# Attention and token mixing: the first batch planned with other durations, priorities and shares of work

## The chip, the cores and the metric

One NeuronCore of a Trainium2 chip runs the whole program. The metric is the device time of one execution in microseconds; lower is better. TensorE (PE) multiplies, with its weight loads (PEld) beside it; VectorE (DVE) and ScalarE (ACT) work on its results, GpSimd (POOL) issues most loads and casts a little, SyncE (SP) issues the remaining loads and the stores.

## The reference

For 4 batches, 8 heads, 768 positions and 64 columns a head, it computes attention with sinks and a window, and puts the result through a token and channel mixer:

```python
scores = scale * np.matmul(q, k.transpose(0, 1, 3, 2))
keep = is_sink | in_window              # 4 sinks; the last 128 positions
a = softmax(np.where(keep, scores, -1e9))
x = np.matmul(a, v)                     # heads side by side: [4, 768, 512]
h = np.maximum(x^T @ w_tok1, 0) @ w_tok2      # 768 -> 256 -> 768
u = x + h^T
out = u + np.maximum(u @ w_ch1, 0) @ w_ch2    # 512 -> 1536 -> 512
```

Inputs and output are float32; the kernel works in bfloat16 and accumulates in float32.

## The kernel before

**Tiling.** Two heads make a pair: 4 pairs a batch, 16 in all, numbered from 0. For a pair, q and k are turned by PE (`turn` in the first batch and for pair 4, `transposed` later) and copied out of PSUM as qT and kT; the four sink columns of k go to kTs (`sink_columns`). `scores` makes the window's scores in three groups a pair, g = 0, 1, 2: two of 512 columns a head and one of 384. ACT takes the exp of each (line 509), giving pT. `score_sinks` makes the sink scores of two pairs at once. `pv` multiplies with v, with a column of ones that gives the row sum; DVE takes the reciprocal (572, 612) and writes x (575, 615).

**Mixing.** Per batch and half of the columns g: `mix_h` (x by w_tok1, then relu to h1T), `mix_u` (h1T by w_tok2, plus x, gives u), `transpose_u` or `turned_u` (u turned to uT). Then `mix_channels`: `v1` (uT by w_ch1, relu, line 122 or 124) and `out_part` (by w_ch2, plus u, line 884, stored).

**Masks.** A score group is masked in one of two ways. By PE: `masked` multiplies a table of 0 and -32768 by the identity into the bank, and the scores accumulate on it. By DVE: after the exp, pT is multiplied by a table of 0 and 1 (line 516), which `keep_masks` makes in four instructions (1005). In the first batch PE masks all groups but group 0 of pair 3.

**u.** In the first batch `mix_u` has two forms as well: with `by_pe`, x is added by a product with the identity, and the result only copied, by ACT or DVE; otherwise DVE adds x while it reads the bank (716). Four of the six pieces of the first batch are `by_pe`.

**Banks.** PSUM has two slots "sc", of two banks each, for scores and for turned q and k, and four single banks "mx" for all else. A slot is free for PE when all its readers are done.

**The order.** Every engine works its queue in order, and the order is written when the program is built, by a planner (`Plan`). Each unit of PE work and each operation (`Op`) has an assumed duration per engine it may run on. The planner keeps a clock per engine, and gives the operation that can start earliest to the engine that would finish it first; between equals `urgent` decides. `SEM` is added behind an operation until its result counts as seen, `PE_OUT` behind a PE unit, `SWITCH` where PE changes between work on half the array and on all of it. In the first batch the lists that `first_attention` returns have priority in their order (`stay` and the 40 ns in line 322 say how much later an item high in the list may start and still be taken first). Behind it, `main` (channel mixing) and `side` (attention and token mixing of the next batch) are woven; `target` says how much of the side must be done at which share of main (0.6 in line 1025). Assumed landings of the first loads stand in `landed(...)` (977, 980, 1009). None of these numbers is in the program that runs: they only decide which engine takes what, the order in each queue, and the bank.

**Bursts.** In the later batches the turning of the next pair's q and k, the scores of group 0 and the sinks' part of the last pair's values stand together as one burst; groups 1 and 2 follow in a second one, with channel mixing as filler between the two.

**Loads.** q and k of pairs 0 to 3 come by SP in float32 and are cast on chip (`cast`); everything else comes by POOL, cast on the way, in one fixed sequence: v of pairs 0 to 2, w_tok1, v of pair 3, w_tok2, then pairs 4 and on, with quarters of w_ch1 and w_ch2 between them.

Of the kernel before, what the change touches and what calls it, by code (L numbers as in the profile page):

```python
# [16 lines left out]
def kernel(  # L17
# [16 lines left out]
    NT = S // P  # L34
# [12 lines left out]
    MASKED_BY_PE = [(p, g) for p in range(NHP) for g in range(NT // 2) if (p, g) != (NHP - 1, 0)]  # L47
# [164 lines left out]
    SEM = 90.0  # L212
    PE_OUT = 190.0
    SWITCH = 95.0
    FIRST = 1800.0
# [22 lines left out]
    class Plan:  # L238
# [71 lines left out]
        def run(self, first, main, side, target):  # L310
# [3 lines left out]
            while any(first) or main or side or self.pending:  # L314
# [4 lines left out]
                if early:  # L319
                    soonest = min(t for t in [tm, ts, *(t for t, _ in early)] if t is not None)  # L320
                    stay = [(t, u) for t, u in early if self.half and u[0].half and t <= soonest + SWITCH]
                    t, u = next((e for e in stay + early if e[0] <= soonest + (SWITCH if e in stay else 40.0)), (None, None))
# [71 lines left out]
    def prepare(p):  # L394
# [4 lines left out]
        def evict(e, n, part):  # L399
# [8 lines left out]
            copy(e, to if parts == 1 else to[:, part], tiles["ps_" + name, p] if parts == 1 else tiles["ps_" + name, p][part])  # L408

        def sink_columns(e):  # L410
            c = ODD * (p % 2)
            first = (tiles["ps_k", p][:, 0] if parts == 1 else tiles["ps_k", p][0])[:, 0, 0:n_sink]
            for i in range(2):
                copy(e, ks[ds(D * i, D), i, c:c + n_sink], first[ds(D * i, D)])

        free = ([("sk", p - 2)] if p >= 2 else [], [("s", p - NKB)] if p >= NKB else [])
        if parts == 2:
            cost = {"DVE": 540.0, "ACT": 500.0}
        else:
            cost = {"DVE": 950.0} if p < NHP else {"DVE": 950.0, "ACT": 900.0}  # L420
        for n, name in enumerate(("qT", "kT")):
# [7 lines left out]
            {"ACT": 440.0, "DVE": 400.0}, sink_columns, [("sk", p - NHP)] if p >= NHP else [],  # L429
        )  # L430

    def turn(p, n):
# [3 lines left out]
        def run():  # L436
            ps = [bank("mx", NT, D, dtype=BF16) for _ in range(2)]
            tiles["ps_" + name, p] = [t.rearrange("d j p -> d p j") for t in ps]
# [47 lines left out]
    def scores(p, g):  # L486
# [32 lines left out]
        x.cost, x.fn, x.deps = {"ACT": 190.0 + 1.5 * width(g)}, exp, [done["pv", p - 2]] if p >= 2 else []  # L519
        x.urgent = 2 * (p < NHP)  # L520
        then = [x]
        if not by_pe:
            then.append(Op({"DVE": 100.0 + 1.2 * width(g)}, mask, [x, done["masks"]]))
# [6 lines left out]
    def score_sinks(p):  # L530
# [13 lines left out]
        x = Op({"ACT": 580.0}, exp, [done["pv", p - 2]] if p >= 2 else [])  # L544
# [6 lines left out]
    def pv(p, half):  # L551
# [29 lines left out]
        r = Op({"DVE": 180.0}, recip)  # L581
        n = Op({"DVE": 550.0}, norm, [r])
        n.urgent = r.urgent = (1 + 1.5 * (p >= NHP // 2)) * (p < NHP)
# [9 lines left out]
    def sink_values(p):  # L593
# [15 lines left out]
        for i in range(2):  # L609
# [10 lines left out]
            done["r", p, i] = Op({"DVE": 180.0}, recip)  # L620
            done["x", p, i] = Op({"DVE": 550.0}, norm, [done["r", p, i]])
# [19 lines left out]
    def sink_rows(p):  # L641
# [5 lines left out]
        done["vs", p] = Op({"ACT": 440.0, "DVE": 400.0}, both, [done["v", p], done["pv", p - NHP]])  # L647
# [422 lines left out]
```

## Time and profile before

| | us |
|---|---|
| median of 3 runs (lowest to highest) | 209.58 (209.21 to 210.65) |
| the profiled execution: time | 209.46 |
| its span, first to last instruction | 207.7 |
| PE busy in the span | 198.0 (95%) |
| DVE busy | 114.3 (55%) |
| ACT busy | 114.4 (55%) |
| POOL busy | 67.5 (32%) |
| w_tok1 landed (first token product at 19.27) | 19.22 |
| last exp of the first batch ends | 22.95 |
| first product with w_ch1 | 30.78 |

The span runs from the first to the last instruction; 1.76 us of the time lie outside it. All later times are microseconds from the start of the span. Busy times of PE are modelled, as matmuls are pipelined: the row of a 256-column product says 0.27 us, but the next one starts 0.11 us later. Where work follows on work, the step from start to start is what an instruction costs its engine, and the row is what its reader waits for. The granted TensorE clock is 0.998 of full speed over the whole span.

### The profile page before, as it was taken

The numbers are of one execution on the slowest core, as the hardware profiler recorded it, in microseconds if no ns is written. First come the engines' busy times: TensorE is split into PE (matmuls) and PEld (weight loads), VectorE is DVE, ScalarE is ACT, GpSimd is POOL, SyncE is SP. The second block draws the span as 40 slices with busy tenths as digits, with TensorE's granted clock in tenths as the row PEclk, the third lists the DMA queues.
The fourth block names the chain that finished last, engine by engine and source line by source line (L and its number), as shares of the span: only waits on it lengthen the run. The fifth ranks groups of instructions, "written<-read, shape, count | busy, mean of one in ns | idle before, by whom it ended". The sixth has DMA issues, their size and how long they took to land.

```text
span 207.7 us, 5034 instructions
## 1 busy us (share of the span) xinstructions
PE 198.0 (95%) x2126; PEld 119.3 (57%) x2145; DVE 114.3 (55%) x252; ACT 114.4 (55%) x202; POOL 67.5 (32%) x86
## 2 busy tenths in 40 slices
PE   6699999999999999999999999999999999999994
PEld 2345975566665665557656645666666445665443
DVE  4786664777577675867576552767674421000222
ACT  4799668878727435867684241868751103774000
POOL 6399759794699980720000000000000000000000
PEclk9999999999999999999999999999999999999999
DMA  6999999999999999795000212100001122000222
GB/s 198 283 260 182 172 174 191 156 164 201 156 159 176 185 206 195 52 70 37 3 0 5 101 51 104 51 5 0 3 0 49 56 101 101 3 0 0 101 104 101
DMA packets 73222, 21.57 MB, mean 104 GB/s; under 512 B 63216, under 2 KB 70256, under 8 KB 73200
## 3 DMA queue, kind: packets, MB, share of 16 engines
q0 software_dynamic: 67232, 11.80, 71.9%
q1 hardware_dynamic: 5968, 9.45, 12.9%
q8 instruction: 17, 0.28, 0.6%
q14 instruction: 5, 0.04, 0.1%
HBM read 26.75 MB, written 6.29 MB: 159 GB/s over the span
## 4 chain that ended last, share of the span: by engine, by line
PE 83%; DMA 6%; DVE 4%; ACT 2%; issue 2%; POOL 1%; SPq 0%; POOLq 0%; DVEq 0%
PE ps_mx L109 75%; PE ps_sc L109 5%; DMA w_tok<-in_moe_w_tok_dram 4%; DMA v_sink_f<-in_v_dram 2%; PE ps_sc L460 2%; DVE x_sb L615 1%; ACT qT L116 1%; DVE kT L118 1%; POOL v_aug L102 1%; PE ps_mx L745 1%; ACT v1T L122 1%; DVE recip L612 1%; PE ps_mx L112 1%; POOL v_sink L118 0%; SPq L188 0%
## 5 line engine op out<-in xcount | busy, mean ns | idle before, releaser
L109 PE MATMUL ps_mx<-uT,w_ch 128*128 128x384 bf16 x384 | 68.3, 326 | 0.9 <-DVE x_sb L615 0.9
L109 PE MATMUL ps_mx<-w_ch,v1T 128*128 128x512 bf16 (+2 forms) x299 | 64.2, 362 | 0.9 <-issue 0.3
L122 ACT ACTIVATE v1T<-ps_mx 128x384 bf16<-128x384 f32 x74 | 36.3, 493 | 33.7 <-PE ps_mx L109 22.9
L109 PEld LDWEIGHTS <-w_ch 128*128 128x128 bf16 x384 | 35.5, 98 | 25.0 <-DVE x_sb L615 2.5
L109 PEld LDWEIGHTS <-v1T 128*128 128x128 bf16 x312 | 28.9, 98 | 29.2
L509 ACT ACTIVATE pT<-ps_sc 128x1024 bf16<-128x1024 f32 (+1 forms) x48 | 44.4, 956 | 2.2 <-PE ps_sc L109 1.9
L884 DVE TENSOR_TENSOR o_sb<-ps_mx,u_sb 128x512 f32<-128x512 f32 x23 | 15.9, 691 | 44.6 <-PE ps_mx L109 44.6
L94 POOL DMA_DIRECT2D q_bf<-in_q_dram x24 | 19.7, 822 | 4.7 <-DMA w_ch<-in_moe_w_ch_dram 2.4
L109 PEld LDWEIGHTS <-w_tok 128*128 128x128 bf16 x192 | 18.3, 98 | 4.8 <-DMA w_tok<-in_moe_w_tok_dram 0.5
L94 POOL DMA_DIRECT2D k_bf<-in_k_dram x24 | 19.6, 820 | 3.1 <-DMA w_ch<-in_moe_w_ch_dram 1.7
L102 POOL DMA_DIRECT2D v_aug<-in_v_dram x16 | 16.4, 1028 | 10.9 <-PE ps_mx L109 8.0
L118 DVE COPY kT<-ps_sc 128x768 bf16<-128x768 bf16 x11 | 10.5, 958 | 17.0 <-ACT qT L116 17.0
L516 DVE TENSOR_TENSOR pT<-pT,mask_main 128x1024 bf16<-128x1024 bf16 (+1 forms) x24 | 14.5, 620 | 3.6 <-ACT pT L509 3.5
L109 PE MATMUL ps_sc<-qT,kT 64*128 64x256 bf16 x192 | 15.5, 262 | 0.3
L109 PE MATMUL ps_mx<-v_aug,pT 128*128 128x65 bf16 x352 | 15.3, 194 | 0.0
L716 DVE TENSOR_TENSOR u_sb<-ps_mx,x_sb 128x512 bf16<-128x512 f32 x20 | 12.7, 685 | 4.2 <-PE ps_mx L109 4.2
L109 PEld LDWEIGHTS <-pT 128*128 128x128 bf16 x352 | 13.5, 97 | 2.0 <-issue 0.6
L124 DVE TENSOR_SCALAR v1T<-ps_mx 128x384 bf16<-128x384 f32 x22 | 12.1, 554 | 2.7 <-PE ps_mx L109 2.0
L109 PE MATMUL ps_mx<-h1T,w_tok 128*128 128x256 bf16 x96 | 12.6, 273 | 0.0
L116 ACT ACTIVATE qT<-ps_sc 128x768 bf16<-128x768 bf16 x11 | 8.9, 810 | 6.4 <-PE ps_sc L460 6.2
L109 PE MATMUL ps_mx<-x_sb,w_tok 128*128 128x256 bf16 x96 | 12.0, 273 | 0.1
L615 DVE TENSOR_TENSOR x_sb<-ps_mx,recip 128x384 bf16<-128x384 f32 x22 | 11.4, 551 | 0.1
(72 smaller groups left out, 152.2 us busy)
## 6 DMA issues: line engine op xcount, KB each, us to landing
out_dram<-o_sb SPq DMA_DIRECT2D x23, 256.0 KB, 2.0
v_aug<-in_v_dram POOLq DMA_DIRECT2D x16, 192.0 KB, 6.5
w_ch<-in_moe_w_ch_dram POOLq DMA_DIRECT2D x8, 384.0 KB, 8.9
q_bf<-in_q_dram POOLq DMA_DIRECT2D x24, 96.0 KB, 6.6
k_bf<-in_k_dram POOLq DMA_DIRECT2D x24, 96.0 KB, 5.6
q_f<-in_q_dram SPq DMA_DIRECT2D x4, 384.0 KB, 5.6
k_f<-in_k_dram SPq DMA_DIRECT2D x4, 384.0 KB, 5.9
w_tok<-in_moe_w_tok_dram POOLq DMA_DIRECT2D x2, 384.0 KB, 8.1
```

Source lines behind the costliest of these rows:

```text
L94: in_order(nc.gpsimd.dma_start(out=out[:, h], in_=rows[:, h]))
L102: in_order(nc.gpsimd.dma_start(out=v_aug.rearrange("p i t d -> p (i t) d")[:, :, 0:D], in_=v[b].rearrange("h s d -> (h s) d")[2 * hp * S:2 ...
L109: in_order(nc.tensor.matmul(*args, skip_group_check=True, **kwargs))
L116: in_order(nc.scalar.activation(out, in_, AF.Copy))
L118: in_order({"DVE": nc.vector, "POOL": nc.gpsimd}[e].tensor_copy(out=out, in_=in_))
L122: in_order(nc.scalar.activation(out, in_, AF.Relu))
L124: in_order(nc.vector.tensor_scalar_max(out=out, in0=in_, scalar1=0.0))
L509: in_order(nc.scalar.activation(part(tiles["pT", p][:, :, ds(2 * g, 2)]), tiles["ps_s", p, g][:, :, 0:width(g)], AF.Exp, scale=scale,))
L516: in_order(nc.vector.tensor_tensor(out=pt, in0=pt, in1=m, op=ALU.mult))
L615: in_order(nc.vector.tensor_tensor(out=x_sb[b][:, :, ds((2 * hp + i) * D, D)], in0=tiles["ps_o", p, i][:, :, 0:D], in1=tiles["recip", p, i ...
L716: in_order(nc.vector.tensor_tensor(out=u_part(b, g, s0, n), in0=tiles["ps_u", b, g, s0], in1=x_sb[b][:, s0:s0 + n, c0:c0 + cn], op=ALU.add,))
L884: in_order(nc.vector.tensor_tensor(out=o_sb.rearrange("p (g c) -> p g c", g=2), in1=u_rows(b, st), in0=tiles["ps_out", b, st].rearrange("p ...
```

## The change

Three things change in what is computed where, all in the first batch:

- DVE masks three groups (pair 2 group 2, pair 3 groups 0 and 2) in place of one; PE masks nine in place of eleven.
- u of the first batch is added by DVE in all six pieces; `mix_u` loses its form with the identity, so four copies that ACT made go too.
- The lists of `first_attention` are returned in another order: the token work of the second half of the columns stands second, ahead of the masks.

All else is numbers of the planner: durations of operations are set to about the step from one instruction to the next (an exp 100 + 1.62 a column for 190 + 1.5, a copy of 384 columns 470 and 400 for 540 and 500), the delay behind an operation grows (`SEM` 165 for 90) and the one behind PE shrinks (`PE_OUT` 45 for 190), a new `STAY` of 250 takes the place of `SWITCH` in the two tests for first lists, urgency of exps and norms is changed, landings of loads are set anew (the tables of `keep_masks` count as ready at 18.0 us for 5.7), and `target` has 0.7 for 0.6. The parts of a turned pair in `tiles` get keys of their own, which changes nothing in the program.

The diff, without the lines around each place:

```diff
@@ line 47 of before @@
-    MASKED_BY_PE = [(p, g) for p in range(NHP) for g in range(NT // 2) if (p, g) != (NHP - 1, 0)]
+    MASKED_BY_DVE = [(NHP - 2, 2), (NHP - 1, 0), (NHP - 1, 2)]
@@ line 212,2 of before @@
-    SEM = 90.0
-    PE_OUT = 190.0
+    SEM = 165.0
+    PE_OUT = 45.0
@@ line 214,0 of before @@
+    STAY = 250.0
@@ line 321,2 of before @@
-                    stay = [(t, u) for t, u in early if self.half and u[0].half and t <= soonest + SWITCH]
-                    t, u = next((e for e in stay + early if e[0] <= soonest + (SWITCH if e in stay else 40.0)), (None, None))
+                    stay = [(t, u) for t, u in early if self.half and u[0].half and t <= soonest + STAY]
+                    t, u = next((e for e in stay + early if e[0] <= soonest + (STAY if e in stay else 100.0)), (None, None))
@@ line 408 of before @@
-            copy(e, to if parts == 1 else to[:, part], tiles["ps_" + name, p] if parts == 1 else tiles["ps_" + name, p][part])
+            copy(e, to if parts == 1 else to[:, part], tiles[("ps_" + name, p) if parts == 1 else ("ps_" + name, p, part)])
@@ line 412 of before @@
-            first = (tiles["ps_k", p][:, 0] if parts == 1 else tiles["ps_k", p][0])[:, 0, 0:n_sink]
+            first = (tiles["ps_k", p][:, 0] if parts == 1 else tiles["ps_k", p, 0])[:, 0, 0:n_sink]
@@ line 418 of before @@
-            cost = {"DVE": 540.0, "ACT": 500.0}
+            cost = {"DVE": 470.0, "ACT": 400.0}
@@ line 420 of before @@
-            cost = {"DVE": 950.0} if p < NHP else {"DVE": 950.0, "ACT": 900.0}
+            cost = {"DVE": 870.0, "ACT": 720.0}
@@ line 429 of before @@
-            {"ACT": 440.0, "DVE": 400.0}, sink_columns, [("sk", p - NHP)] if p >= NHP else [],
+            {"ACT": 340.0, "DVE": 310.0}, sink_columns, [("sk", p - NHP)] if p >= NHP else [],
@@ line 438 of before @@
-            tiles["ps_" + name, p] = [t.rearrange("d j p -> d p j") for t in ps]
+            for x in range(2):
+                tiles["ps_" + name, p, x] = ps[x].rearrange("d j p -> d p j")
@@ line 519,2 of before @@
-        x.cost, x.fn, x.deps = {"ACT": 190.0 + 1.5 * width(g)}, exp, [done["pv", p - 2]] if p >= 2 else []
-        x.urgent = 2 * (p < NHP)
+        x.cost, x.fn, x.deps = {"ACT": 100.0 + 1.62 * width(g)}, exp, [done["pv", p - 2]] if p >= 2 else []
+        x.urgent = 3 * (p < NHP)
@@ line 523 of before @@
-            then.append(Op({"DVE": 100.0 + 1.2 * width(g)}, mask, [x, done["masks"]]))
+            then.append(Op({"DVE": 110.0 + 0.94 * width(g)}, mask, [x, done["masks"]]))
@@ line 544 of before @@
-        x = Op({"ACT": 580.0}, exp, [done["pv", p - 2]] if p >= 2 else [])
+        x = Op({"ACT": 510.0}, exp, [done["pv", p - 2]] if p >= 2 else [])
@@ line 581,3 of before @@
-        r = Op({"DVE": 180.0}, recip)
-        n = Op({"DVE": 550.0}, norm, [r])
-        n.urgent = r.urgent = (1 + 1.5 * (p >= NHP // 2)) * (p < NHP)
+        r = Op({"DVE": 110.0}, recip)
+        n = Op({"DVE": 470.0}, norm, [r])
+        n.urgent = r.urgent = 2 * (p < NHP)
@@ line 620,2 of before @@
-            done["r", p, i] = Op({"DVE": 180.0}, recip)
-            done["x", p, i] = Op({"DVE": 550.0}, norm, [done["r", p, i]])
+            done["r", p, i] = Op({"DVE": 110.0}, recip)
+            done["x", p, i] = Op({"DVE": 470.0}, norm, [done["r", p, i]])
@@ line 647 of before @@
-        done["vs", p] = Op({"ACT": 440.0, "DVE": 400.0}, both, [done["v", p], done["pv", p - NHP]])
+        done["vs", p] = Op({"ACT": 340.0, "DVE": 310.0}, both, [done["v", p], done["pv", p - NHP]])
@@ line 691 of before @@
-            {"ACT": 190.0 + 0.78 * w, "DVE": 150.0 + 1.05 * w},
+            {"ACT": 100.0 + 0.79 * w, "DVE": 60.0 + 1.06 * w},
@@ line 699 of before @@
-    def mix_u(b, g, s0, n, by_pe=False):
+    def mix_u(b, g, s0, n):
@@ line 705,2 of before @@
-                if by_pe:
-                    mm(ps_u[:, st], ident, x_sb[b][:, s0 + st, c0:c0 + cn], start=True, stop=False)
@@ line 710 of before @@
-                        start=(tt == 0 and not by_pe), stop=(tt == NTOK - 1),
+                        start=(tt == 0), stop=(tt == NTOK - 1),
@@ line 714,2 of before @@
-            if by_pe:
-                return copy(e, u_part(b, g, s0, n), tiles["ps_u", b, g, s0])
@@ line 720 of before @@
-        op = Op({"DVE": 150.0 + 1.05 * n * cn}, add)
+        op = Op({"DVE": 60.0 + 1.06 * n * cn}, add)
@@ line 722,2 of before @@
-        if by_pe:
-            op.cost["ACT"] = 190.0 + 0.78 * n * cn
@@ line 725 of before @@
-        return unit(n * (NTOK + by_pe) * cn * 0.422, run, done["h", b, g] + [done["tok2"]], {"mx": [[op]]}, [op])
+        return unit(n * NTOK * cn * 0.422, run, done["h", b, g] + [done["tok2"]], {"mx": [[op]]}, [op])
@@ line 754 of before @@
-            ops.append(Op({"ACT": 900.0, "DVE": 950.0}, evict))
+            ops.append(Op({"ACT": 720.0, "DVE": 870.0}, evict))
@@ line 771 of before @@
-            {"ACT": 190.0 + 0.78 * w, "DVE": 150.0 + 0.52 * w},
+            {"ACT": 100.0 + 0.79 * w, "DVE": 60.0 + 0.53 * w},
@@ line 790 of before @@
-                if (p, g) in MASKED_BY_PE:
+                if (p, g) not in MASKED_BY_DVE:
@@ line 802 of before @@
-            tokens[g] += [mix_u(0, g, st, 2, g == 0 or st == 2) for st in range(0, NT, 2)]
+            tokens[g] += [mix_u(0, g, st, 2) for st in range(0, NT, 2)]
@@ line 804 of before @@
-        return scored, masks, turned, out, *tokens[::-1]
+        return scored, tokens[1], masks, tokens[0], turned, out
@@ line 864 of before @@
-                {"ACT": 490.0, "DVE": 550.0},
+                {"ACT": 400.0, "DVE": 460.0},
@@ line 896 of before @@
-                done["o", b, st] = Op({"DVE": 690.0}, add)
+                done["o", b, st] = Op({"DVE": 600.0}, add)
@@ line 945 of before @@
-        return Op({"POOL": 1750.0}, lambda e: load_cast(p, n), free, lag=1500.0, loads=2)
+        return Op({"POOL": 1650.0}, lambda e: load_cast(p, n), free, lag=1500.0, loads=2)
@@ line 951 of before @@
-        return Op({"POOL": 1070.0}, load, [("pv", p - NV)] if p >= NV else [], lag=1600.0, loads=1)
+        return Op({"POOL": 1010.0}, load, [("pv", p - NV)] if p >= NV else [], lag=1600.0, loads=1)
@@ line 957 of before @@
-    plan.free.update(PE=3000.0, ACT=2200.0, DVE=3900.0, POOL=4100.0)
+    plan.free.update(PE=4700.0, ACT=2200.0, DVE=3500.0, POOL=4700.0)
@@ line 974 of before @@
-        cost = {"POOL": 850.0} if p == NHP - 1 else {"DVE": 570.0} if p or n else {"ACT": 850.0}
+        cost = {"POOL": 850.0} if p == NHP - 1 else {"DVE": 470.0} if p or n else {"ACT": 740.0}
@@ line 977 of before @@
-    for p, at in enumerate(((3900.0, 5300.0), (7500.0, 8600.0), (11300.0, 12500.0), (13500.0, 14700.0))):
+    for p, at in enumerate(((3850.0, 5400.0), (7300.0, 8400.0), (10900.0, 12200.0), (13200.0, 14400.0))):
@@ line 980 of before @@
-    v_sink = Op({"POOL": 650.0}, lambda e: copy(e, v_sink0, v_sink_f), [landed(9000.0)])
+    v_sink = Op({"POOL": 650.0}, lambda e: copy(e, v_sink0, v_sink_f), [landed(8600.0)])
@@ line 1009 of before @@
-    done["masks"] = Op({"DVE": 1300.0}, keep_masks, [landed(5700.0)])
+    done["masks"] = Op({"DVE": 1300.0}, keep_masks, [landed(18000.0)])
@@ line 1025 of before @@
-            f = m / msize / 0.6
+            f = m / msize / 0.7
```

What the build makes of it, by the order of the instructions on each engine: PE has 12 matmuls less (eight products of x with the identity, four of mask_add with 384 columns). POOL and SP have the same instructions in the same order. In the first batch, six copies of qT and kT go from ACT to DVE and two pairs of kTs copies from DVE to ACT; the four instructions of `keep_masks` move on DVE from behind the first cast to behind the last kTs of the batch; q of pair 2 is turned ahead of a mask instead of behind it, and the first half of pair 0's values stands ahead of the scores of pair 1 group 1; the first `mix_h` stands as one piece of 12 products behind the first half of pair 3's values, where before it stood in two pieces around pair 2's; one unit of v1 comes ahead of pair 4's turning. Later, the bursts stand behind other amounts of v1 (pair 5's behind 24 products for 16, pair 6's behind 64 for 52), the distance between a pair's two bursts is four products shorter for pairs 5, 7, 10 and 14, and in these four ACT makes kTs right behind qT, where before DVE made it.

## The prediction

> **What bounds the kernel now.** I read the page's busy row first (PE 198.0 of 207.7 us), then busy time by stretches, then the chain that ended last, then the waits. A table of stretches (columns: stretch, its length, busy time and instructions of PE, PEld, DVE, ACT, POOL, granted clock, DMA share, GB/s):
>
> ```profile
> 5.00:19.20 14.20, 11.81 (x206) 6.27 (x203) 11.19 (x31) 12.61 (x21) 10.74 (x13) 1.00 1.59 249
> 19.20:30.50 11.30, 11.08 (x147) 9.25 (x146) 6.47 (x15) 7.81 (x13) 7.80 (x10) 1.00 1.90 176
> ...
> 80.00:160.00 80.00, 78.67 (x911) 49.18 (x915) 50.30 (x107) 46.96 (x84) 5.27 (x6) 1.00 0.26 39
> ```
>
> To 19.2 us nobody is full: PE idles 2.4 us, ACT 1.6. From there PE is the bound: 0.2 us idle up to 30.5, where the first product with w_ch1 could start, and only some 2.5 us in the 177 us behind it. The chain of work agrees:
>
> ```profile
> 11.33 7.89 DMA w_tok<-in_moe_w_tok_dram
> 19.22 0.05 issue
> 19.27 0.83 PE ps_mx L109 x6
> 20.10 1.25 PE ps_sc L109 x12
> 21.34 5.84 PE ps_mx L109 x88
> ```
>
> The first stage hangs on the landing of w_tok1 at 19.22, then on PE's own work. So an edit is worth the PE time it takes out behind 19.2, or what it adds in PE waits. Loads set a floor: the first quarter of w_ch1 is issued at 19.7 and takes 8.4 us, landing at 28.1. POOL's order is unchanged instruction by instruction, so these times stay.
>
> The waits show a second thing, needed below (engine waiting, for whom: us in total, times, longest):
>
> ```profile
> DVE kT L118 <- ACT qT L116: 17.0, 11, 2.3
> ACT kTs L116 <- DVE kT L118: 7.5, 8, 1.0
> ```
>
> In all eleven later pairs DVE copies kT only once ACT has copied qT from the same bank, and kTs comes after both.
>
> **What goes.** The build's list has 12 matmuls less, all in the first batch.
> - Eight identity products for u. In the timeline one begins at 23.75 and the next matmul at 23.85; the next pair is 24.07 and 24.18. 8 x 0.11 = 0.87 us, all in the full stretch.
> - Four mask products of 384 columns, 0.16 us each (pairs of them stand 0.3 apart): 0.65 us. Half of it belongs to pair 2, at 17.0, where PE still waits for others, and counts nothing; pair 3's counts 0.32.
>
> Together 1.2 us off a PE that is full.
>
> **What moves in the attention of the first batch.** ACT hands six copies (0.39 us step) to DVE and takes two pairs of kTs (0.35): 1.6 us less before its last exp. Does that bring exps forward? Up to group 1 of pair 1, no: q of pair 2 lands at 10.67, its DVE cast takes 0.95 in its row, so it is turned by 12.2; then stand in PE's new order a mask (0.43), a PV half now put ahead of the scores (0.38) and the scores (0.44 to their reader). The exp begins near 13.2 against 13.28 before. From there ACT has three copies less, and I carry its last exp to 21.9 instead of 22.95. That alone is worth little: behind 20.2 PE is full in both. In the new order PE still has there 1.84 us of PV (four halves, 0.38 or 0.54 each), 48 token products of 0.109 (5.2) and 24 transposes of 0.055 (1.3): 8.4 us, to 28.6.
>
> **What the adds cost.** u was copied four times by ACT and added twice by DVE; now DVE adds six times, in a 0.60 us step (two at line 716 take 1.28: 0.59 + 0.69). PE makes the three pieces of the second half in 0.43 steps, so DVE falls behind: first one ready near 27.0, third added at 28.9, four transposes and their latency to 29.2, an eviction of 0.4 to 0.6, and v1 begins near 29.6. Before, it could have begun at 30.5 (at 30.78, but with 0.28 of pair 4's transposes ahead, which now follow). **First stage: -0.9 us** out of the 1.2 removed; the rest is PE waiting for adds. Bounds: if DVE's later masks (0.9 us at 18 us, two more mask products of 0.55) push its norms back by as much, nothing is left (0); if v1 starts as w_ch1 lands, -2.4.
>
> DVE's casts are where this could slip: k of pair 2 is now cast at 13.1, where POOL casts q of pair 3 (13.18 in the trace), and this trace has the same cast at 0.56 alone and 0.95 beside POOL's work. The Trainium skill (SBUF — State Buffer, "Who interferes with whom") says why: GpSimd's port is VectorE's second one, held for a whole instruction, so one of them blocks. By that rule the cast costs 0.4 more and the sum would be 209.5; by the short row it is 209.1.
>
> **What the planner's new numbers do later.** It has shorter evictions, a longer stay in half-array work and a later target (0.7): bursts come after other amounts of filler, and kTs of pairs 5, 7, 10 and 14 goes from DVE to ACT, ahead of an exp. But kTs waits for kT and kT for qT, about 1 us in which ACT, in order, does nothing; exp and the v1 evictions queue behind it. Pair 8 shows the full chain now, with its burst at 59.41:
>
> ```profile
> 60.04 0.81 ACT L116 ACTIVATE qT<-ps_sc 128x768 bf16<-128x768 bf16 x1 [3.93 <-PE ps_sc L460]
> 61.88 0.35 ACT L116 ACTIVATE kTs<-ps_sc 64x4 bf16<-64x4 bf16 x2 [1.02 <-DVE kT L118]
> 62.25 1.02 ACT L509 ACTIVATE pT<-ps_sc 128x1024 bf16<-128x1024 f32 x1
> ```
>
> The exp frees its bank at 63.27, 3.9 us after the burst began; the last scores of the second burst need that bank. PE loses what its own work falls short of 3.9. Pair 5 in the new order: burst 0.68, twelve v1 products of 0.162 (1.95), sink scores 0.43, first scores 0.25: 3.3, so it waits 0.6. Before, with kTs on DVE, exp ended at 36.81 and PE came at 37.68: no wait. Pairs 10 and 14 fall short by 0.2 each, pair 12 by 0.2 for an eviction; pair 7 waits 0.4 as it did (0.39). Sum 0 to 1.2. I take pair 5's and leave out the small ones, as pair 8's own row shows no wait of that size: **+0.5**.
>
> The Trainium skill (PSUM — Partial Sum Buffer, "PSUM bank collisions raise a hardware error") says that two engines may not touch one bank and quadrant at once, so dependencies must keep even two readers apart. By that rule the 17.0 us of waits stay in the new kernel, and the trace agrees in 11 of 11 pairs; by the planner's costs, which let kT run beside qT, this term would be 0 and the sum 208.6.
>
> **Sum.** -0.9 + 0.5 = -0.4. Profiled execution: span 207.7, time 209.46, 1.76 outside the span (taken as fixed); it lies 0.1 under the median of 209.58. Forecast 209.46 - 0.4 = **209.1 us**: no change that shows. About 1% (2.1 us) is what a measurement of this kernel can tell from no change.
>
> **Rivals.**
> - *Faster: the first stage goes down to its loads* (0.25). v1 starts at 28.1, -2.4 us, and the later waits of PE (0.24 to 0.39, some 1.7 in all) go down as the plan fits better, offsetting pair 5: 209.46 - 2.4 = 207.1. For: ACT is 89% full up to 19.2 and loses 1.6 us. Pairs 5 and 6 leave room: their k land at 32.7 and 40.4, used at 34.05 and 41.7, and the new order puts 8 and 12 v1 products more ahead of them. Against: the adds, one after another.
> - *Slower: ACT parked in the bursts* (0.15). With ACT away for 1 us, two v1 results sit in the four mx banks beside two PV results, and PE also waits for an eviction, a whole v1 unit (0.65) per place: 4 x 0.65 = 2.6, with the 1.2 above 3.8; less 0.9: 212.4. It decides where PE has more than two units between a burst and the first DVE norm (3.1 us behind the burst). For: 0.24 us waits of that kind at 44.7 and 103.4. Against: DVE now takes a v1 eviction right behind kT in two of the four.
> - *DVE becomes the first stage's bound* (inside the forecast's 0.6): 11.19 busy of 14.2 us, plus six copies of 0.47, less 0.9 of masks and 0.65 of kTs is 12.5, in order. First stage 0: 209.46 + 0.5 = 210.0.
> - *The edits do nothing to the order*: excluded by the build's list.
>
> **Range and chances.** Forecast 0.6, within 1% with the rivals near it; 0.25 faster by over 1%; 0.15 slower. The range takes in the fast rival's 207.1 and the bounds 0 and +1.2 (210.7), with some of the slow one: 207.0 to 211.2.
>
> **What would show it.** Right: the first v1 product near 29.6; three adds back to back on DVE with PE waiting some 0.6 us before it; exp of pair 4, group 0 ending 3.9 us behind pair 5's burst and PE waiting there. Wrong: v1 before 28.8 or behind 30.5; no wait at pair 5; PE idle behind 38 us above 4 us; or k of pair 5 landing after PE asks for it.

## The result, and the profile after

The changed kernel takes **212.45 us** (median of 4 runs, 211.86 to 212.99) against 209.57 (209.21 to 210.65) for the kernel before on the same chip: a ratio of 1.0125, interval 1.0104 to 1.0146. It is slower by some 2.9 us, where the forecast was 209.1. Its profiled execution took 212.66 us, span 210.8 (before 209.46 and 207.7).

Busy time hides the loss. This is the busy row of the page, then the table of stretches, whose first two and last rows answer those shown of before:

```profile
PE 201.0 (95%) x2133; PEld 120.2 (57%) x2133; DVE 117.0 (55%) x242; ACT 112.6 (53%) x214; POOL 67.9 (32%) x86
```

```profile
5.00:19.20 14.20, 12.78 (x203) 7.05 (x199) 11.15 (x27) 10.12 (x18) 9.68 (x11) 1.00 1.55 242
19.20:30.50 11.30, 11.23 (x143) 8.89 (x144) 10.66 (x27) 6.84 (x12) 9.28 (x12) 1.00 1.86 178
...
80.00:160.00 80.00, 77.97 (x899) 48.22 (x897) 49.75 (x97) 47.76 (x94) 5.28 (x6) 1.00 0.28 41
```

PE is still 95% busy and has 3.0 us more busy time, though the program has 12 matmuls less. From 38 to 200 us its idle time is 3.21 us, against 2.48 before: 0.7 more, while far more was lost there. The chain that ended last tells more. Here are its pieces (start, length, what) around the end of the first batch and around pair 5's first burst:

```profile
27.14 0.70 DVE u_sb L714 x2
...
28.41 0.69 DVE u_sb L714
...
34.91 0.49 ACT v1T L122
35.40 0.79 ACT qT L116
...
36.21 0.97 DVE kT L118
...
37.58 1.03 ACT pT L511
...
38.65 0.34 PE ps_sc L109 x4
```

Before, PE made up 83% of the chain, and between 21.34 and 41.61 us only one add by DVE (0.70) stood in it; now PE has 74% and ACT 12%. In the first batch the chain runs through DVE's adds, and then through the copies of one burst: qT, kT, exp. The two waits shown of before answer like this:

```profile
DVE kT L118 <- ACT qT L116: 14.5, 11, 2.8
ACT kTs L116 <- DVE kT L118: 11.6, 12, 1.0
```

ACT now waits 11.6 us for kT: in all eleven later pairs, and once at pair 4 (0.4).

**Where the 3.2 us went.** For every group of PE instructions behind the first w_ch1 product I compared the time to the next group with the steps of its instructions where nothing waits (a v1 product, uT by w_ch1, 0.1625 us, a w_ch2 product 0.216, a sink product 0.215, a score 0.058, a product with values 0.0305, a 64x64 transpose 0.0155). What is over is waiting, also where PE counts as busy. Summed from the first w_ch1 product on, it is 4.79 us before and 7.96 after: +3.17. Of that, +2.95 lies **between the first and the second burst of a pair** (2.98 before, 5.93 after); between a second burst and the next first one, beyond the bursts themselves, it is 1.14 and 1.18. Against it stands the first w_ch1 product, at 30.04 for 30.78 (-0.74; 0.2 of it only because a transpose group of pair 4 now follows, where it is paid again). The last store's landing in this one execution adds 0.48. -0.74 + 0.2 + 3.17 + 0.48 = 3.1, the difference of the spans.

Pair 5 shows how it is made. The timeline of PE and ACT (start, length, engine, line, what; in brackets the idle time before and what ended it):

```profile
34.80 0.35 PE L462 MATMUL ps_sc<-ident,q_bf 64*128 64x64 bf16 x12
...
35.16 0.38 PE L109 MATMUL ps_sc<-qT,kT 64*128 64x256 bf16 x4
35.48 2.12 PE L109 MATMUL ps_mx<-uT,w_ch 128*128 128x384 bf16 x12
37.44 0.59 PE L109 MATMUL ps_mx<-qT,kTs 128*128 128x512 bf16 x2
37.97 0.39 PE L109 MATMUL ps_sc<-qT,kT 64*128 64x256 bf16 x4
38.65 0.34 PE L109 MATMUL ps_sc<-qT,kT 64*128 64x256 bf16 x4 [0.29 <-ACT pT L511]
38.93 2.77 PE L109 MATMUL ps_mx<-uT,w_ch 128*128 128x384 bf16 x16
...
35.37 0.81 ACT L116 ACTIVATE qT<-ps_sc 128x768 bf16<-128x768 bf16 x1
37.21 0.35 ACT L116 ACTIVATE kTs<-ps_sc 64x4 bf16<-64x4 bf16 x2 [1.02 <-DVE kT L118]
37.58 1.02 ACT L511 ACTIVATE pT<-ps_sc 128x1024 bf16<-128x1024 f32 x1
```

The same place in the kernel before: four more v1 products ahead of the last eight scores, and no wait for the exp.

```profile
36.94 0.81 PE L109 MATMUL ps_mx<-uT,w_ch 128*128 128x384 bf16 x4
37.68 0.56 PE L109 MATMUL ps_sc<-qT,kT 64*128 64x256 bf16 x8
...
34.49 0.81 ACT L116 ACTIVATE qT<-ps_sc 128x768 bf16<-128x768 bf16 x1
...
35.79 1.02 ACT L509 ACTIVATE pT<-ps_sc 128x1024 bf16<-128x1024 f32 x1
```

In the changed kernel the work from burst to burst is 24 x 0.0155 + 4 x 0.058 + 12 x 0.1625 + 2 x 0.215 = 2.98 us; with the second burst's eight scores (0.46) it is 3.45, and 38.93 - 34.80 = 4.13 passed: 0.68 of waiting (0.20 before). ACT stands idle 1.02 us for kT, and the exp that frees the bank ends 3.2 us after qT began. In the kernel before it ended 2.3 to 2.5 us after it in four pairs, those with kTs on DVE, and 3.2 in seven; now 3.2 to 3.7 in all eleven.

The table gives, for the pairs whose waiting or work changed most, PE's work between its two bursts and the waiting there (us):

| pair | 5 | 6 | 7 | 9 | 11 | 12 | 15 |
|---|---|---|---|---|---|---|---|
| before, work | 3.63 | 3.47 | 3.90 | 9.74 | 3.25 | 4.12 | 3.25 |
| before, waiting | 0.20 | 0.49 | 0.43 | 0 | 0.49 | 0.40 | 0.49 |
| after, work | 2.98 | 3.47 | 3.25 | 9.74 | 3.25 | 4.12 | 3.90 |
| after, waiting | 0.68 | 0.58 | 0.89 | 0.17 | 1.19 | 0.49 | 1.36 |

### The profile page after: what moved, and what is told of

Same layout as the page of the kernel before. It is cut to its first block, busy times and chain, and to the rows that moved or that the text cites. A ratio compares the mean times of both kernels' runs of the same rounds, so it can differ in the third digit from the quotient of the medians.

```text
span 210.8 us, 5028 instructions
## 1 busy us (share of the span) xinstructions
PE 201.0 (95%) x2133; PEld 120.2 (57%) x2133; DVE 117.0 (55%) x242; ACT 112.6 (53%) x214; POOL 67.9 (32%) x86
## 4 chain that ended last, share of the span: by engine, by line
PE 74%; ACT 12%; DVE 5%; issue 2%; ACTq 0%; DVEq 0%
PE ps_mx L109 66%; PE ps_sc L109 5%; ACT pT L511 4%; ACT v1T L122 3%; ACT qT L116 3%; DVE kT L118 3%; PE ps_mx L741 1%; PE ps_mx L444 1%; ACT kTs L116 1%; ACT v_sink L116 1%; DVE u_sb L714 1%; PE ps_sc L462 1%; DVE x_sb L617 1%; PE ps_mx L112 0%; DVE recip L614 0%
## 5 line engine op out<-in xcount | busy, mean ns | idle before, releaser
L109 PE MATMUL ps_mx<-uT,w_ch 128*128 128x384 bf16 x384 | 69.2, 326 | 0.7 <-DVE v1T L124 0.3
L109 PE MATMUL ps_mx<-w_ch,v1T 128*128 128x512 bf16 (+2 forms) x312 | 66.0, 363 | 0.0
L122 ACT ACTIVATE v1T<-ps_mx 128x384 bf16<-128x384 f32 x76 | 36.9, 494 | 32.0 <-PE ps_mx L109 22.2
L109 PEld LDWEIGHTS <-v1T 128*128 128x128 bf16 x312 | 28.8, 98 | 28.8
L714 DVE TENSOR_TENSOR u_sb<-ps_mx,x_sb 128x512 bf16<-128x512 f32 x24 | 15.6, 686 | 12.0 <-PE ps_mx L109 12.0
L118 DVE COPY kT<-ps_sc 128x768 bf16<-128x768 bf16 x11 | 10.5, 958 | 14.5 <-ACT qT L116 14.5
L518 DVE TENSOR_TENSOR pT<-pT,mask_main 128x768 bf16<-128x768 bf16 (+1 forms) x26 | 15.6, 616 | 3.9 <-ACT pT L511 3.8
L109 PE MATMUL ps_sc<-qT,kT 64*128 64x256 bf16 x192 | 16.3, 268 | 0.6 <-ACT pT L511 0.6
L109 PEld LDWEIGHTS <-pT 128*128 128x128 bf16 x352 | 14.0, 98 | 2.6 <-issue 0.3
L124 DVE TENSOR_SCALAR v1T<-ps_mx 128x384 bf16<-128x384 f32 x20 | 10.9, 553 | 3.1 <-PE ps_mx L109 3.0
L109 PEld LDWEIGHTS <-kT 64*128 64x128 bf16 x192 | 7.3, 96 | 8.9 <-issue 7.3
```

The lines of the kernel that those rows point to most:

```text
L109: in_order(nc.tensor.matmul(*args, skip_group_check=True, **kwargs))
L118: in_order({"DVE": nc.vector, "POOL": nc.gpsimd}[e].tensor_copy(out=out, in_=in_))
L122: in_order(nc.scalar.activation(out, in_, AF.Relu))
L124: in_order(nc.vector.tensor_scalar_max(out=out, in0=in_, scalar1=0.0))
L518: in_order(nc.vector.tensor_tensor(out=pt, in0=pt, in1=m, op=ALU.mult))
L714: in_order(nc.vector.tensor_tensor(out=u_part(b, g, s0, n), in0=tiles["ps_u", b, g, s0], in1=x_sb[b][:, s0:s0 + n, c0:c0 + cn], op=ALU.add,))
```

## The experiments

Each is the changed kernel with one edit, unless said otherwise. The ratios are against the kernel before, run on the same chip in the same sitting; the last two columns are of one profiled execution each. The theories of the first four: **A**, bursts planned too close for the chain qT, kT, kTs, exp, because of the shorter durations; **B**, the target of 0.7; **C**, the first batch's edits; **K**, ScalarE standing behind kT is the whole loss.

| | median us | ratio (interval) | first w_ch1 product | waiting between a pair's bursts |
|---|---|---|---|---|
| before | 209.57 | 1 | 30.78 | 2.98 |
| changed | 212.45 | 1.0125 (1.0104 to 1.0146) | 30.04 | 5.93 |
| e1 target 0.6 | 213.40 | 1.0158 (1.0134 to 1.0183) | 30.92 | 5.44 |
| e2 kTs by DVE | 211.54 | 1.0069 (1.0047 to 1.0091) | 30.19 | 4.26 |
| e3 order of the readers told | 208.04 | 0.9891 (0.9850 to 0.9931) | 30.25 | 0.67 |
| e4 old numbers later | 209.42 | 0.9986 (0.9962 to 1.0010) | 29.94 | 2.69 |
| e5 order told, kernel before | 208.17 | 0.9919 (0.9898 to 0.9941) | 31.20 | 1.01 |
| e6 u by the identity | 212.78 | 1.0140 (1.0112 to 1.0167) | 30.74 | 5.77 |
| e7 copies planned long | 209.52 | 0.9983 (0.9959 to 1.0007) | 30.62 | 1.99 |
| e8 exps planned long | 212.18 | 1.0112 (1.0079 to 1.0146) | 30.63 | 5.29 |
| e9 copies long, kTs by ACT | 209.15 | 0.9964 (0.9936 to 0.9991) | 29.97 | 2.19 |
| e10 masks by PE | 215.06 | 1.0254 (1.0216 to 1.0291) | 32.75 | 6.79 |
| e11 e3 again | 206.94 | 0.9863 (0.9837 to 0.9889) | 28.77 | 0.68 |
| e12 masks by PE, old lists | 214.18 | 1.0203 (1.0176 to 1.0231) | 32.81 | 5.72 |

### e1: the target back

```diff
-            f = m / msize / 0.7
+            f = m / msize / 0.6
```

> The changed kernel with the share of main at which the side must be done put back from 0.7 to 0.6, nothing else. Theory A (the later stages lose because bursts stand too close for the chain qT, kT, kTs, exp, and that comes from the shorter durations): the order hardly moves, the shortest distances between bursts stay (3.0 us for pair 5, 2.4 us between second and next first burst), so 212.3, within 0.5 of the changed kernel's 212.45. Rival B (the later target moves the side work badly): 210.0 or less. Rival C (the first batch's edits cost the time): 212.4.

Nothing came back, so B falls. The target moves the bursts from pair 12 on only. The time is 0.95 us above the changed kernel's, more than the 0.5 that A allowed; the intervals of the two ratios overlap, so no loss is shown, and the profiled execution was late by 0.88 at the first w_ch1 product already, where the edit changes nothing.

### e2: kTs by VectorE alone

```diff
-            {"ACT": 340.0, "DVE": 310.0}, sink_columns, [("sk", p - NHP)] if p >= NHP else [],
+            {"DVE": 310.0} if parts == 1 else {"ACT": 340.0, "DVE": 310.0}, sink_columns,
+            [("sk", p - NHP)] if p >= NHP else [],
```

> The changed kernel with the sink columns kTs of pairs 6 and on copied by VectorE alone. Rival K (ScalarE parked behind kT is the whole loss): exps come 1 us earlier in every burst, 209.5 to 210.3. Theory A (distance): the wait for the exp's bank goes, but norms stand 0.3 us later on VectorE and the bursts are as close, so PE waits for x_sb instead: 211.5 to 212.5. Rival C: 212.4.

The edit holds for pairs 5 to 15 (the expectation counts pairs from 1). In all eleven the exp now ends 1.7 us after qT began, sooner than in any pair of the kernel before, and yet half of the loss stays (4.26 us of waiting). K as the whole loss does not fit, and A's range (211.5 to 212.5) is met. At pairs 7, 11 and 15 PE still waits for x_sb (0.51, 0.51 and 0.44 us).

### e3: the planner told what waits for what

```diff
+        if parts == 1:
+            done["kT", p][0].deps.append(done["qT", p][0])
+            done["kTs", p].deps.append(done["kT", p][0])
```

> The changed kernel, where the planner is told for the later pairs what the traces show: kT waits for qT, kTs for kT. No instruction is added or taken away. Theory A: distances from first to second burst grow to 3.9 us and more, PE's waits there (0.3 to 0.9 us at pairs 5, 7, 11, 15) mostly go; some remain where a second burst and the next first one stand 2.4 us apart: 209.5 to 210.5. Rival C: 212.4.

The running program keeps this order already (kT waits for qT in 11 of 11 pairs); now the planner counts it. The loss went, and with it most of the waits that the kernel before had: 208.04 us beats both kernels, and lies below the 209.5 to 210.5 that A gave.

### e4: the first batch as changed, the later ones with the old numbers

```diff
+    late = [False]
+    def num(then, now):
+        return then if late[0] else now
...
-            cost = {"DVE": 870.0, "ACT": 720.0}
+            cost = {"DVE": num(950.0, 870.0), "ACT": num(900.0, 720.0)}
...
     first = first_attention()
+    late[0] = True
```

All durations on ACT and DVE that the later batches use, both delays and the target are treated so.

> The changed kernel in the first batch; for all that is planned behind it the old durations, delays and target. Theory A: the later stages take what they took before (177.2 us from the first possible v1 product to the end of the span) and the first stage keeps its gain of 0.5 us: 208.6 to 209.3, at or under the kernel before. Rival C (the first batch's edits cost the time): 212 or more.

The time of before returns. The loss comes from the numbers used behind the first batch, not from the first batch, whose edits are worth about 0.3 us here (the interval reaches to a gain of 0.8 and a loss of 0.2).

### e5: the order told to the kernel before

The three lines of e3, in the kernel before (they hold for pairs 5 to 15).

> The kernel before, with nothing changed but that the planner is told, for pairs 4 and on, that kT waits for qT and kTs for kT. Theory A (PE waits wherever two bursts stand closer than the chain qT, kT, kTs, exp needs, and the planner does not know that chain): the distances from first to second burst grow from 3.3 to 4.1 us or more in eight of eleven pairs, so most of before's own waits of PE behind 38 us (4.8 us over what its instructions step, against 2.6 in the kernel with both) should go: about 1.5 us less, 208.1 us, ratio 0.993. Rival P: before's longer durations already keep the bursts apart well enough, and the order only repairs what the change broke: 209.6 us, ratio 1.000.

208.17, as A had it (208.1). Before's own waits were of the same kind, and P falls.

### e6: u by products with the identity

```diff
-            tokens[g] += [mix_u(0, g, st, 2) for st in range(0, NT, 2)]
+            tokens[g] += [mix_u(0, g, st, 2, g == 0 or st == 2) for st in range(0, NT, 2)]
```

with before's second form of `mix_u`.

> The changed kernel with u of the first batch as before: four of six pieces add x by a product with the identity and are copied by ScalarE or VectorE. All distances between later bursts stay within one product group of the changed kernel's. By the prediction's terms: 8 identity products of 0.11 us come back (+0.87) and PE no longer waits for VectorE's adds (-0.46 measured): +0.4, 212.9 us, ratio 1.015. Rival Q: the adds cost PE as much as the products did, since VectorE is late in this stretch: 212.4 us or less, ratio 1.0125 or below.

+0.33 us against the changed kernel by the medians, where +0.4 was expected; the intervals overlap, so the size is consistent but not shown, and Q is not excluded.

### e7 and e8: which durations

e7, the later pairs' copies:

```diff
-            cost = {"DVE": 870.0, "ACT": 720.0}
+            cost = {"DVE": 950.0, "ACT": 900.0}
...
-            {"ACT": 340.0, "DVE": 310.0}, sink_columns, [("sk", p - NHP)] if p >= NHP else [],
+            {"ACT": 440.0, "DVE": 400.0} if parts == 1 else {"ACT": 340.0, "DVE": 310.0}, sink_columns, [("sk", p - NHP)] if p >= NHP else [],
```

> The changed kernel, but the later pairs' copies out of PSUM are planned with before's durations (qT and kT 950 and 900, kTs 400 and 440). In the built order the kTs of pairs 5, 7, 10 and 14 go back to VectorE and the distance from first to second burst is longer in four pairs (3.64 for 2.99 at pair 5); the distances from a second burst to the next first one stay mostly short (2.42 at pairs 11 and 15). Theory A (two separate losses, one per kind of distance): about 1.3 of 3.0 us come back, 211.1 us, ratio 1.006. Rival K (ScalarE standing behind kT for kTs is the whole loss): 209.5 us, ratio 0.999.

e8, the later pairs' exps:

```diff
-        x.cost, x.fn, x.deps = {"ACT": 100.0 + 1.62 * width(g)}, exp, [done["pv", p - 2]] if p >= 2 else []
+        x.cost, x.fn, x.deps = {"ACT": 100.0 + 1.62 * width(g) if p < NHP else 190.0 + 1.5 * width(g)}, exp, [done["pv", p - 2]] if p >= 2 else []
```

> The changed kernel, but the exps of the later pairs are planned with before's duration (190 + 1.5 a column for 100 + 1.62). In the built order the distance from a second burst to the next first burst grows from 2.41 to 3.06 us at pairs 7, 11 and 15; kTs stays on ScalarE in all eleven pairs and pair 5's two bursts stay 2.99 apart. Theory A: the waits for x_sb and v1T at those three places (0.73, 0.73 and 0.92 us with what stands beside them) fall to before's 0.33 to 0.40, so 1.2 to 1.6 us come back: 211.0 us, ratio 1.006. Rival K: the loss stays, 212.4 us, ratio 1.0125.

e7 alone takes the whole loss away, and e8 gives nothing that can be measured: A in the form of two separate losses falls, and these two numbers are K's. The distance from a second burst to the next first one matters only a little (waiting at pairs 11 and 15 falls from 1.19 and 1.36 to 0.95 each in e8). But e7 did several things at once: kTs went to DVE in four pairs (5, 10, 12 and 14, where 5, 7, 10 and 14 were expected), and the distance between a pair's bursts grew in three (5, 7 and 11). e9 parts them.

### e9: long distances, kTs on ScalarE everywhere

e7 with kTs given `{"ACT": 440.0}` alone for the later pairs.

> The changed kernel with the later pairs' copies planned long (qT and kT 950 and 900, kTs 440), but kTs given to ScalarE alone. In the built order ScalarE makes kTs in all eleven pairs, as in the changed kernel, while PE's work between a pair's two bursts is as long as where the copies were planned long (3.64, 3.47 and 3.90 us for pairs 5 to 7) or longer (4.77, 3.89, 5.42, 4.76 for pairs 10, 11, 12, 14, where the changed kernel has 3.47, 3.25, 4.12, 3.47). Theory D (PE loses what its work between the two bursts falls short of the chain, so the distance decides and the engine of kTs adds a little): waits between the bursts 1.5 to 2.5 us against 5.93 in the changed kernel, 209.2 us, ratio 0.998. Rival K (ScalarE standing behind kT is what costs, at any distance): waits of 4 us or more, 211.5 us or above, ratio 1.008 or above.

The chain is as long as in the changed kernel, with the exp at the same place, though at pair 5 a v1 eviction now fills part of ACT's wait for kT:

```profile
35.31 0.81 ACT L116 ACTIVATE qT<-ps_sc 128x768 bf16<-128x768 bf16 x1
36.27 0.49 ACT L122 ACTIVATE v1T<-ps_mx 128x384 bf16<-128x384 f32 x1 [0.16 <-PE ps_mx L109]
37.14 0.35 ACT L116 ACTIVATE kTs<-ps_sc 64x4 bf16<-64x4 bf16 x2 [0.38 <-DVE kT L118]
37.52 1.02 ACT L511 ACTIVATE pT<-ps_sc 128x1024 bf16<-128x1024 f32 x1
...
35.41 2.77 PE L109 MATMUL ps_mx<-uT,w_ch 128*128 128x384 bf16 x16
```

But PE has sixteen products ahead for twelve, and at pair 5 it waits 0.20 us for 0.68. The time is 209.15 us: D holds and K falls. With e2 it makes a square, by the waiting between bursts: short distances with kTs on ACT 5.93, short with kTs on DVE 4.26, long with kTs on ACT 2.19, long with kTs mostly on ACT (e7) 1.99. The distance is the larger lever; the engine of kTs counts where the distance is short.

It is not the only one, as the planner lays all later work anew with each edit. Pair 15 has the same work between its bursts in e7 and e9 as in the changed kernel (3.90), the same 2.41 ahead of its first burst, and kTs on ACT; but no v1 eviction stands between kTs and the exp there any more (in e7 DVE makes two, at 136.93 and 137.93), and the waiting falls from 1.36 to 0.35 and 0.53. Of the 3.94 us of waiting that e7 takes away, 1.0 is this pair's, and 2.0 that of pairs 5, 7 and 11, whose distance grew (pair 5's kTs went to DVE as well).

### e10 and e12: the masks

e10:

```diff
-    MASKED_BY_DVE = [(NHP - 2, 2), (NHP - 1, 0), (NHP - 1, 2)]
+    MASKED_BY_DVE = [(NHP - 1, 0)]
```

> The changed kernel with masks as before: PE masks group 2 of pairs 2 and 3 again (four products of 384 columns more, 0.65 us), VectorE only group 0 of pair 3. Distances between the later bursts as in the changed kernel. By the prediction's terms half of the 0.65 lies where PE waits for others anyway: +0.3, 212.7 us, ratio 1.014, first product with w_ch1 0.3 us later. Rival V (VectorE is what the end of the first stage hangs on: freed of two mask products, 0.9 us, it adds u earlier): 0 or a gain, 212.1 us, ratio 1.011.

e12 has the same, and the lists in before's order:

```diff
-        return scored, tokens[1], masks, tokens[0], turned, out
+        return scored, masks, turned, out, *tokens[::-1]
```

> The changed kernel with masks as before (PE masks group 2 of pairs 2 and 3 again) and with the lists of the first batch in the order of before. In the built order the token work of the second half of the columns no longer stands ahead of pair 3's last values, pair 4 is turned just ahead of the first product with w_ch1, and the distances between the later bursts are those of the changed kernel. Theory S (the masks on PE cost only their own products, and what went wrong with masks by PE alone was the order that the new lists then give: token work drawn ahead, so that the first half's additions and transposes stood between the values): first product with w_ch1 about 1.9 us earlier than there, near 30.9, 212.9 us, ratio 1.015. Rival M (the masks on PE cost 2.6 us by themselves, since each waits for a bank that an exp has yet to free): 215 us, ratio 1.025.

Neither came as expected. e10 loses 2.6 us against the changed kernel, all of it ahead of or in pair 5 (first w_ch1 product at 32.75). e12 still loses 1.7, between S (212.9) and M (215), so the order of the lists explains about a third by the medians; the intervals of e10 and e12 overlap a little. The timeline of e12 shows what goes on late in the batch:

```profile
22.38 0.48 PE L109 MATMUL ps_sc<-mask_add,ident 128*128 128x384 bf16 x2 [0.41 <-ACT pT L511]
...
21.30 1.02 ACT L511 ACTIVATE pT<-ps_sc 128x1024 bf16<-128x1024 f32 x1 [0.90 <-PE ps_mx L109]
22.22 0.59 ACT L544 ACTIVATE pT_sink<-ps_mx 128x512 bf16<-128x512 f32 x1
22.70 1.74 ACT L511 ACTIVATE pT<-ps_sc 128x1024 bf16<-128x1024 f32 x2
```

The mask product is the first that needs the bank, so PE waits 0.41 us for the exp that frees it, as M has it. ACT's own wait of 0.90 is for something else: the values of pair 1, for which the exps of pair 3 wait (line 521). From 21.30 on ACT has no gap, and its last exp ends at 24.44, against 22.82 in the changed kernel. In e10, where the same two waits stand (0.42 and 0.91), it ends at 23.09, only 0.27 later, and the first w_ch1 product is late all the same. By the steps of its instructions, PE waits 1.6 us from 15 us to that product in the changed kernel, 4.8 in e10 and 3.1 in e12, the longest stretch of it in e12 at the transposes of u (1.10, against 0.46). So more than the masks' own PE time is lost, but these rows do not show that the masks' banks are what costs it: each edit also gives the rest of the batch another order. The kernel before, with the same masks on PE as e10 and e12, had its last exp done at 22.95. Why its other numbers cope with them was not tried.

### e11: e3 once more

> The changed kernel with the planner told that kT waits for qT and kTs for kT in the later pairs, again, with more rounds, to set it against the kernel before with the same order told (208.17 us, ratio 0.9919). If the first batch's edits are worth the 0.4 us that the prediction gave them once the later bursts are right: ratio 0.990. If they are worth nothing: 0.992 or more.

0.9863, a larger gain than expected, and clear of e5's interval (the first run of the same program, e3, was not): with the bursts right, the rest of the change is worth something, 0.3 to 0.6% by the two runs (0.9891 and 0.9863 against 0.9919). This is the fastest version, faster than both kernels. What the planner makes of the order shows on ACT and PE at pair 5 (the three added lines move the exp to line 514):

```profile
33.53 0.35 PE L465 MATMUL ps_sc<-ident,q_bf 64*128 64x64 bf16 x12
34.21 3.42 PE L109 MATMUL ps_mx<-uT,w_ch 128*128 128x384 bf16 x20
38.00 0.56 PE L109 MATMUL ps_sc<-qT,kT 64*128 64x256 bf16 x8
...
34.10 0.81 ACT L116 ACTIVATE qT<-ps_sc 128x768 bf16<-128x768 bf16 x1
34.81 1.02 ACT L514 ACTIVATE pT<-ps_sc 128x1024 bf16<-128x1024 f32 x1
...
36.76 0.34 ACT L116 ACTIVATE kTs<-ps_sc 64x4 bf16<-64x4 bf16 x2
```

The exp goes right behind qT, ACT idles for nobody's kT, kTs comes when kT is long done, and PE gets twenty products for twelve. Its second burst shows no wait.

## Why the prediction was wrong

**The step that failed is the term for the planner's numbers later: +0.5, where the runs show about +3.** Its chain was there: kTs sits on ACT in all eleven pairs, the exp of pair 4 ends 3.8 us behind pair 5's burst, and pair 5 waits 0.68 us in all for a forecast of 0.6. The wait that it priced, the last scores waiting for the exp's bank, is the one that counts at pair 5 alone (0.29 of idle time there); at the other costly places PE waits for what stands behind that chain, x_sb or a v1 eviction. Place by place:

- The step "pair 8's own row shows no wait of that size" took pair 8 (work 3.46, waiting 0.15 in both kernels) as the rule for the rest, and set "pairs 10 and 14" and "pair 12" at nothing. For these three that was right: together they added 0.2.
- "Pair 7 waits 0.4 as it did" was wrong: its distance fell from 3.90 to 3.25, and it waits 0.89. The list did not price what follows kT on DVE, the norms of x, for which PE waits at the sink scores (0.57).
- Pairs 11 and 15 are not in the list at all, and they make more than half of what was lost between the bursts (+0.70 and +0.87 of 2.95). Their distances had not shrunk (3.25 and 3.90, for 3.25 twice). But their first burst now comes 2.41 us of work behind the last second one, for 3.71. So its scores already wait for a bank, and behind the two exps that they wait for, two v1 evictions stand on ACT ahead of qT. At pair 11 PE then waits 0.57 us for x_sb. Pair 15 in the changed kernel has a v1 eviction behind kTs as well:

```profile
137.44 0.39 PE L109 MATMUL ps_sc<-qT,kT 64*128 64x256 bf16 x4 [0.18 <-ACT pT L511]
...
140.79 0.59 PE L109 MATMUL ps_mx<-qT,kTs 128*128 128x512 bf16 x2 [0.76 <-ACT v1T L122]
...
139.88 0.35 ACT L116 ACTIVATE kTs<-ps_sc 64x4 bf16<-64x4 bf16 x2 [1.02 <-DVE kT L118]
140.25 0.49 ACT L122 ACTIVATE v1T<-ps_mx 128x384 bf16<-128x384 f32 x1
```

The sink scores need one of the four mx banks, and the v1 eviction that frees one is parked behind kTs; where it is gone from there, in e7 and e9, most of pair 15's waiting goes too. That is the wait of the **rival that was given 0.15, ACT parked in the bursts**. Its 212.4 is the measured time, but not by its sum: it had four places at a v1 unit each, and it named pairs 5, 7, 10 and 14 by way of kTs, where the runs show waits grown at nine places, the large ones at pairs 11 and 15, and the distance as the larger lever.

**The first stage: -0.9.** The first w_ch1 product came at 30.04, for a forecast of 29.6. Two of the terms that this was carried from had moved: the last exp ends at 22.82 for 21.9, and the loads did not stay (w_tok1 lands at 19.78 for 19.22, the first quarter of w_ch1 at 28.70 for 28.1), though PE waits for neither load. The fast rival's 28.1 was not reached, though e11, where nothing below collided, came to 28.77. Counted by the 30.50 that the prediction set for the kernel before, that is -0.46, about half. Over nine profiled executions with the same order of PE up to there it comes at 28.77 to 30.92, 30.15 in the mean. The adds are as foretold: DVE falls behind, with PE waiting 0.46 us for them at the transposes (0.6 forecast). Of the terms, the identity products and the adds agree with e6, whose size is not clear of noise. The masks do not: 0.32 was set for them, and e10 and e12 lose 2.6 and 1.7 us when they go back to PE. The prediction counted their PE time alone. What the rest is, the bank that they wait for or the order that the planner then gives to all else, is open; so is why the first batch gains so little in all (e4), since the kernel before has these masks on PE and no such loss.

**The two rules of the Trainium skill.** The waits of kT for qT stay in the changed kernel (14.5 us), in 11 of 11 pairs, as the Trainium skill (PSUM — Partial Sum Buffer, "PSUM bank collisions raise a hardware error") has it: two readers of a bank are kept apart. The prediction used the rule to keep its term, and e3 shows what it is worth to let a planner know it: 4.4 us between the changed kernel and e3, by the medians. For the cast of k of pair 2 the prediction chose the short row against the rule of the Trainium skill (SBUF — State Buffer, "Who interferes with whom"); in the changed kernel's own profile the short row came (0.55), but in five of nine executions of this order the rule was the better guide (below).

**What would show it.** Of the signs named, v1 between 28.8 and 30.5, the adds back to back and the wait at pair 5 all came as for a right forecast, and PE's idle time behind 38 us stayed under 4. That sign was a bad one: of 3.2 us lost, 0.7 showed as idle.

## What to carry to other kernels

In this kernel, durations alone do not describe a chain of readers: a planner that knows an operation's length, but not that it must wait for another reader of the same bank, puts too little work behind a burst, and durations that are too long can hide it (e7). Count waiting as elapsed time less the steps of the work, since PE's busy share can stand still (95% in both) and its idle time grow by 0.7 us only, while 3 us are lost. And when a row shows that a step fits, price every place where it occurs with what stands ahead of it in the queue, not the place that looks most like the one row at hand.

## What was not expected of the hardware

**A cast beside GpSimd's cast.** The change puts DVE's cast of k of pair 2 where POOL casts q of pair 3. In the changed kernel's own profile DVE's starts 0.2 us first and takes what it takes alone; POOL's starts inside it and is the longer one:

```profile
14.14 0.55 DVE L118 CAST k_bf<-k_f 128x768 bf16<-128x768 f32 x1
...
14.35 1.02 POOL L118 CAST q_bf<-q_f 128x768 bf16<-128x768 f32 x1 [1.02 <-DMA q_f<-in_q_dram]
```

In e2 POOL's starts 0.02 us first, DVE's is the longer one, and PE waits for the result:

```profile
13.02 1.91 DVE L118 CAST k_bf<-k_f 128x768 bf16<-128x768 f32 x1
...
13.00 0.86 POOL L118 CAST q_bf<-q_f 128x768 bf16<-128x768 f32 x1
...
14.98 0.35 PE L445 MATMUL ps_mx<-ident,k_bf 64*128 64x64 bf16 x12 [1.34 <-DVE k_bf L118]
```

Among the nine executions with this order DVE's cast takes 0.55 to 0.71 us in four and 1.27 to 1.91 in five (e1, e2, e3, e4, e7), and in these five PE waits 0.70 to 1.34 us for it. In the five POOL starts first, by 0.01 to 0.09 us. In the four DVE starts first or level (the changed kernel, e8, e9 and e11), and POOL's cast takes 0.94 to 1.23 for the 0.84 it has elsewhere. This agrees with the exclusive port on the page SBUF — State Buffer of the Trainium skill ("Who interferes with whom"): whoever issues first holds it for the whole instruction. The 1.27 is no longer than POOL's cast and DVE's own one after the other (0.86 + 0.55); the 1.80 of e1 and the 1.91 are longer, and no run here shows why. The longest, 1.91 for 0.55, costs more than three times what the prediction allowed for it (0.4).

**A slow start of PE that the clock row does not show.** In six of the fourteen profiled executions (the changed kernel's, e1, e5, e7, e8 and e12) PE works at half pace until some 9.8 us or later. The same four mask products, in the changed kernel and in the kernel before:

```profile
6.84 1.89 PE L109 MATMUL ps_sc<-mask_add,ident 128*128 128x512 bf16 x4
```

```profile
6.68 1.04 PE L109 MATMUL ps_sc<-mask_add,ident 128*128 128x512 bf16 x4
```

The granted clock of that stretch is 1.00 in both profiles. With the same order of PE, the first w_ch1 product comes at 30.55 us in the mean of four such executions and at 29.82 in the mean of the other five. That is 0.7 us, but the two sets overlap (30.04 to 30.92 and 28.77 to 30.25) and the casts above differ as well, so the cost is not shown. The Trainium skill (TensorE: Matmul & The Clock Gate, Part 1) tells of a clock at half rate until PE has been busy for a window of time; that fits the pace, and no row here shows the gate itself.
